# Fused attention, token-mixing MLP and residual on one core: order of the first loads, last transposes by halves, and a new table of dispatch tolerances

## The chip, the cores and the metric

The kernel runs on one core of a Trainium2 chip. The metric is the device time of one execution in microseconds (us). TensorE (PE in the profile) multiplies matrices, VectorE (DVE), ScalarE (ACT) and GpSimd (POOL) work elementwise, and SyncE (SP) issues most of the transfers; ScalarE issues a few. Each engine runs its own instructions in order and waits on semaphores for the others.

## The reference

```python
x = A_x                                  # 1 x 2048 x 512, bf16
xn = layernorm(x)
# A: attention, 32 heads of 16
q, k, v = split(xn @ wqkv)
p = softmax(q k^T / 4)
A = (p v) @ wo
# B: mixing along the 2048 tokens, F = 1376
h = layernorm(xn)
u = gelu(einsum("bsd,sf->bdf", h, w1) + b1)
B = transpose(einsum("bdf,fs->bds", u, w2) + b2)
out = x + A + B
```

## The kernel before

**Blocks and groups.** Attention is cut into 32 blocks: four blocks of 512 queries times eight sets of four heads. The four heads of a set share the 128 partitions, 32 rows each. A block runs over 16 key tiles of 128 keys, and one block with one key tile is a group, so there are 512 groups. For a group TensorE computes four score tiles, keys on the partitions and 512 queries along the free dimension, one PSUM bank per head (`score_mm`, L653).

**Two ways to the exponential.** ScalarE takes two heads at a time: one exponential of 128x1024 from two banks into a buffer `pT` (`exp_tile`, L661). VectorE has an approximation in integer arithmetic: four conversions of 128x512, one per head (`dve_first`, L708), then two "planes" of 128x2048, shifted copies of the first (`add_plane`, L713). The value products (`pv_mm`, L673) add a group into PSUM bank 6 as four matmuls for a group of ScalarE, twelve for a group of VectorE. The planes of VectorE's groups live in buffers that other work has left free: parts of `x_sb`, `xn_sb`, `xnT`, `wqkv_sb` and a buffer `plx`.

**Planning on the host.** The program is a list scheduler in Python. It keeps a model time for every engine and lets engines choose their next piece of work: `pe_step` for TensorE (scores for ScalarE if a pair of banks is nearly free, scores for VectorE, else `pe_fill`: value products "P", or pieces of projections and MLP "F"), `dve_step` for VectorE, `misc_step` for the others. Which engine takes a group comes out of this: `act_fetch` gives it to ScalarE, `d_fetch` to VectorE. The result is a fixed order for each engine, with semaphores where one depends on another. Twelve numbers steer the choices, for instance `TOL` (how much a filler on TensorE may overrun the time at which ScalarE's banks come free), `JOIN` and `DEFER` (whether VectorE's scores join ScalarE's, or TensorE waits for that), and `D_LAST` (until when VectorE may take groups of the last block). `POLICY` (L93) has 68 rows of them, one for each 10 us of model time.

**Head.** x is loaded in four single tiles of 128 rows (`NPRE`), in turn on the queues of SP and ScalarE, then in larger pieces on SP. `ld_w` (L478) loads weights: the first 128 columns of K (from SP), Q (from ScalarE) and V, later the rest. A small activation on ScalarE brings its table in. TensorE runs eleven products of zeros (`zeros`, L772) from the start. VectorE computes mean and variance of a tile (`ln_stats0` L525, `ln_aggr` L529), GpSimd the reciprocal root (`ln_stats2`: L541, then the power L543). Tile 0 is normalised by ScalarE (`ln_norm_act`, L547): GpSimd first computes its bias `r2` (L548), then ScalarE runs L550. Tiles 1 to 3 are normalised by VectorE (L559). TensorE transposes each tile (`transpose_mm`, L727), ScalarE or VectorE copies it to `xnT` (L588, L590), and K and Q of the four tiles are computed with 128-wide products (L594). ScalarE copies Q in four pieces (L614). After that the first scores and exponentials run, and the remaining twelve tiles follow in the gaps.

**Middle.** Projections, the first MLP product (L962), one GELU on ScalarE (L984), the second MLP product (L993) and the output projection (L1003) fill TensorE between scores and value products. At the end of a block VectorE copies the sums out (L1204), and their reciprocals go through DRAM back to all partitions.

**Tail.** The last block is finished on chip (`tail_epilogue`, L1848), in two halves of 256 columns, so that the output projection of a half can begin early. Each half has four VectorE steps: a transpose from bank 6 (L1862), a reciprocal (L1864), a product (L1866) and a transpose back (L1869). After a half, TensorE adds what that half opens to the last four output tiles (`op_half`, L1011); ScalarE or VectorE copies those out and they are stored. Products that do not depend on the last block wait in `tail["steps"]` and are put on TensorE where the model has room before the end of the half's last transpose.

Of the kernel before, what the change touches and what calls it, by code (L numbers as in the profile page):

```python
# [19 lines left out]
NT = S // 128  # L20
# [44 lines left out]
class Op:  # L65
# [25 lines left out]

SEG = 10000.0
POLICY = [  # L93
# [245 lines left out]
def bass_parallel_sum__softmax_full_mha__mixer_token_mlp__prompt_kernel(  # L339
# [11 lines left out]
    x = A_x  # L351
# [6 lines left out]
    with ExitStack() as es:  # L358
# [119 lines left out]
        def ld_w(j, T0_, T1_, lat, q="act"):  # L478
            c0, c1 = j * D + 128 * T0_, j * D + 128 * T1_
            dma(q, wqkv_sb[:, j, :, 128 * T0_:128 * T1_],  # L480
                A_wqkv[:, c0:c1].rearrange("(ct p) n -> p ct n", p=128),
                reads=[], writes=[("wqkv", j, T) for T in range(T0_, T1_)], name="ld_wqkv", lat=lat)

        for t in range(NPRE):
            dma(("sp", "act")[t % 2], x_sb[:, t, :], x2[128 * t:128 * t + 128, :], reads=[("ident",)] if t == 1 else [],
                writes=[("x", t)], name="ld_x", lat=2150 + 150 * t)
        ld_w(1, 0, 1, 3000, "sp")
        ld_w(0, 0, 1, 3100)
        sc.add("act", lambda e: e.activation(r2[:, 0:1], zw[:, 0:1], ACTF.Identity), reads=[("zw",)], writes=[("r2",)],
               occ=1500)  # L490
# [1483 lines left out]
```

## Time and profile before

| what | value |
|---|---|
| time, median of 3 runs | 691.82 us (690.92 to 692.32) |
| the profiled execution's own time | 693.56 us |
| its span in the profile | 691.5 us |
| busy: ScalarE / VectorE / TensorE / GpSimd | 675.3 / 661.2 / 652.0 / 68.6 us |
| exponentials on ScalarE (L661) | 720, 660.8 us busy |
| conversions on VectorE (L708), planes (L713) | 608, 304 |
| first exponential starts, last one ends | 14.25 us, 682.8 us |
| first transpose of the tail | 684.83 us |

Times are from the start of the span. An instruction's time in the profile can overlap the next one of the same engine, since the engines are pipelined. In a row of the timeline the first number is the start, the second the duration of the merged instructions, and the bracket at the end gives the engine's idle time before it and what released it. TensorE's granted clock reads 1.0 in all stages.

### The profile page before, as it was taken

Reading aid. Unit: us, or ns where it says so; the run is one execution under the profiler, and the core shown is the slowest. Engines: PE = TensorE matmul, PEld = TensorE weight load, DVE = VectorE, ACT = ScalarE, POOL = GpSimd, SP = SyncE. Lnnn points to the kernel's source line nnn. Section 1 sums busy time; section 2 is a strip of 40 time slices with the busy share of each in tenths; the row PEclk is TensorE's granted clock in tenths of the full one; section 3 lists DMA queues with packets and bytes.
Section 4 is the critical chain, followed back from the end, with each engine's and each line's share of the span. In section 5 each row is a group of like instructions: output and inputs, shape, how many; then the busy total and the mean of one; then the engine's idle time right before and its main releaser. Section 6 shows DMA issues by size and latency. Waiting matters only on the chain.

```text
span 691.5 us, 15523 instructions
## 1 busy us (share of the span) xinstructions
PE 652.0 (94%) x6197; PEld 201.6 (29%) x6285; DVE 661.2 (96%) x1159; ACT 675.3 (98%) x737; POOL 68.6 (10%) x100
## 2 busy tenths in 40 slices
PE   8999999999999999999999999999988999999987
PEld 4543333222222222222222222222222222222221
DVE  5988999999999999999999999999999999999997
ACT  4999999999999999999999999999999999999995
POOL 4620100000000000000000001000000000002010
PEclk9999999999999999999999999999999999999999
DMA  8024100122212211220022202211120122212001
GB/s 243 2 50 71 35 12 18 28 48 57 53 36 56 48 43 36 48 50 15 24 49 52 56 24 59 54 51 32 50 52 25 47 57 67 59 41 70 18 7 46
DMA packets 78367, 32.65 MB, mean 47 GB/s; under 512 B 63004, under 2 KB 74204, under 8 KB 78296
## 3 DMA queue, kind: packets, MB, share of 16 engines
q1 hardware_dynamic: 77336, 31.14, 18.7%
q8 instruction: 49, 0.80, 0.5%
q10 hardware_dynamic: 960, 0.52, 0.3%
q14 instruction: 22, 0.18, 0.1%
HBM read 26.08 MB, written 2.61 MB: 41 GB/s over the span
## 4 chain that ended last, share of the span: by engine, by line
ACT 86%; PE 9%; DVE 3%; DMA 1%; issue 1%; POOL 0%; POOLq 0%; DVEq 0%
ACT pT L661 84%; PE ps L673 3%; PE ps L653 3%; PE ps L962 1%; DVE plx L708 1%; ACT gT L984 1%; PE ps L993 1%; DVE x_sb L713 1%; DVE x_sb L708 1%; DMA x_sb<-in_A_x_dram 1%; PE ps L594 0%; PE ps L727 0%; DMA den_scr<-OT 0%; DMA den_s<-den_scr 0%; PE ps L1003 0%
## 5 line engine op out<-in xcount | busy, mean ns | idle before, releaser
L661 ACT ACTIVATE pT<-ps 128x1024 bf16<-128x1024 f32 x720 | 660.8, 1140 | 0.7 <-PE ps L653 0.6
L653 PE MATMUL ps<-QT,KT 32*128 32x512 bf16 x2048 | 288.3, 384 | 24.5 <-ACT pT L661 21.2
L708 DVE TENSOR_SCALAR plx<-ps 128x512 int16<-128x512 f32 x356 | 232.9, 679 | 5.5 <-PE ps L653 4.3
L708 DVE TENSOR_SCALAR x_sb<-ps 128x512 int16<-128x512 f32 x248 | 168.7, 683 | 7.0 <-PE ps L653 0.3
L653 PEld LDWEIGHTS ps<-QT,KT 32*128 32x128 bf16 x2048 | 73.1, 91 | 268.4 <-ACT pT L661 254.0
L673 PE MATMUL ps<-pT,V 128*32 128x512 bf16 x1440 | 142.5, 390 | 0.6 <-DVE V L590 0.3
L713 DVE TENSOR_SCALAR x_sb<-plx 128x2048 int16<-128x2048 int16 x143 | 96.2, 681 | 0.6 <-PE ps L673 0.2
L673 PE MATMUL ps<-plx,V 128*32 128x512 bf16 x624 | 60.4, 382 | 0.1
L673 PEld LDWEIGHTS ps<-pT,V 128*32 128x32 bf16 x1440 | 36.4, 93 | 80.3 <-issue 75.7
L673 PE MATMUL ps<-x_sb,V 128*32 128x512 bf16 x580 | 56.1, 382 | 0.4 <-DVE OT L1204 0.4
L1241 POOL TENSOR_TENSOR oT<-OT,denb 128x512 bf16<-128x512 f32 x16 | 20.3, 1271 | 335.4 <-DVE x_sb L713 188.7
L673 PE MATMUL ps<-x_sb,V17b 128*32 128x512 bf16 x532 | 52.2, 382 | 0.3 <-issue 0.3
L962 PE MATMUL ps<-h_sb,w1blk 128*128 128x512 bf16 (+1 forms) x152 | 49.8, 387 | 2.2 <-issue 2.2
L993 PE MATMUL ps<-gT,w2blk 128*128 128x512 bf16 (+1 forms) x151 | 49.0, 385 | 2.1 <-issue 1.9
L713 DVE TENSOR_SCALAR x_sb<-x_sb 128x2048 int16<-128x2048 int16 x72 | 49.4, 688 | 0.7 <-PE ps L673 0.7
L1241 POOL TENSOR_TENSOR otmp<-OT,denb 128x512 bf16<-128x512 f32 x15 | 19.1, 1273 | 247.4 <-DVE x_sb L713 128.2
L594 PE MATMUL ps<-xnT,wqkv_sb 128*128 128x512 bf16 (+1 forms) x169 | 37.9, 324 | 1.7 <-issue 1.4
L713 DVE TENSOR_SCALAR plx<-x_sb 128x2048 int16<-128x2048 int16 x51 | 34.7, 681 | 0.1
L713 DVE TENSOR_SCALAR plx<-plx 128x2048 int16<-128x2048 int16 x33 | 22.4, 680 | 0.1
L594 PE MATMUL ps<-wqkv_sb,xnT 128*128 128x128 bf16 x256 | 21.1, 220 | 0.0
L1204 DVE COPY OT<-ps 128x512 f32<-128x512 f32 x31 | 21.0, 677 | 0.0
L673 PEld LDWEIGHTS ps<-plx,V 128*32 128x32 bf16 x624 | 16.9, 96 | 12.9 <-issue 7.2
(96 smaller groups left out, 297.6 us busy)
## 6 DMA issues: line engine op xcount, KB each, us to landing
denb<-rec_scr SPq DMA_DIRECT2D x124, 64.0 KB, 2.1
w1blk<-in_B_w_dram SPq DMA_DIRECT2D x10, 512.0 KB, 4.2
w2blk<-in_B_w_dram SPq DMA_DIRECT2D x16, 320.0 KB, 3.7
xres<-in_A_x_dram SPq DMA_DIRECT2D x16, 128.0 KB, 2.3
QT<-qst SPq DMA_DIRECT2D x120, 16.0 KB, 1.8
out_dram<-osb SPq DMA_DIRECT2D x14, 128.0 KB, 1.7
wqkv_sb<-in_A_wqkv_dram SPq DMA_DIRECT2D x3, 384.0 KB, 7.8
x_sb<-in_A_x_dram SPq DMA_DIRECT2D x2, 512.0 KB
```

The costliest lines, as they stand in the source:

```text
L594: return sc.add("pe", lambda e: e.matmul(dst, lhsT=lhsT, rhs=rhs, start=(ct == 0), stop=(ct == NCT - 1)), reads=reads, writes=[("bank", bk ...
L653: return sc.add("pe", lambda e: e.matmul(bank(bk), lhsT=KT[32 * r:32 * r + 32, T, 128 * kt:128 * (kt + 1)], rhs=QT[32 * r:32 * r + 32, slo ...
L661: return sc.add("act", lambda e: e.activation(pT[:, buf, :], ps[:, slot * 1024:(slot + 1) * 1024], ACTF.Exp, scale=EXP_SCALE), reads=[("ba ...
L673: return sc.add("pe", lambda e: e.matmul(bank(PV_BANK)[32 * r:32 * r + 32, :], lhsT=vt_[:, off:off + 32], rhs=rhs, start=start, stop=stop, ...
L708: return sc.add("dve", lambda e: e.tensor_scalar(plane_i[pb][:, 512 * r:512 * (r + 1)], bank(bk), BIAS, 0.0, ALU.add, ALU.max), reads=[("b ...
L713: return sc.add("dve", lambda e: e.tensor_scalar(plane_i[pb], plane_i[pb0], float(SHIFT[j]), BITS_MAX, ALU.add, ALU.min), reads=[("pl", pb ...
L962: op = sc.add("pe", lambda e: e.matmul(bank(xb)[0:m, :], lhsT=w1blk[:, slot, st, 0:m], rhs=h_sb[:, st, :], start=(st == 0), stop=(st == NT ...
L984: op = sc.add("act", lambda e, m=m, f0=f0, f1=f1: e.activation(gT[0:m, f0:f1, :], gT[0:m, f0:f1, :], ACTF.Gelu_apprx_tanh), reads=[("gT", ...
L993: op = sc.add("pe", lambda e: e.matmul(bank(xb), lhsT=w2blk[0:m, slot, ft, :], rhs=gT[0:m, ft, :], start=first, stop=last), reads=([("w2bl ...
L1204: op = sc.add("dve", lambda e: e.tensor_copy(OT32[:, eb, :], bank(PV_BANK)), reads=[("bank", PV_BANK)], writes=[("OT32", eb)], **T_DVE(512))
L1241: op = sc.add("pool", lambda e: e.tensor_tensor(dst, OT32[:, eb, :], denb[:, :], ALU.mult), reads=[("OT32", eb)] + [("denb", r) for r in r ...
```

## The change

In the head, the first two tiles of x are loaded on SP's queue and the next two on ScalarE's. The first K weights follow on SP and wait there until tile 0 has arrived (a read of tile 0 is named as a dependency); the first Q weights come behind them on SP, no longer on ScalarE's queue. GpSimd's bias and ScalarE's norm of tile 0 are put ahead of the statistics of tile 1 in the engines' orders; the model's duration of that norm is 700 instead of 560 ns.

In the tail, the four VectorE steps run half by half in turn: both transposes, both reciprocals, both products, both transposes back. Buffers' keys are renamed accordingly.

In the planner, all rows of `POLICY` are replaced and get a thirteenth number, `SEED`; 38 of 68 rows have one that is not zero. A function `vary(j)` makes a fixed pseudo-random number between -1 and 1 from the seed, the count of exponentials so far and j. It shifts `TOL` by up to 50 ns, `JOIN` by up to 40 and `DEFER` by up to 100, and where `vary(3)` is over 0.6 (one time in five), a value product is ranked behind projection and MLP pieces in `pe_fill`. With seed 0 it gives 0.

```diff
 POLICY = [
-    (115.0, 80.0, 250.0, -1, 0, 1300.0, 0.0, 0.05, 2, 3, 2, 7500.0),
-    (90.0, 30.0, 150.0, -1, 0, 900.0, 0.0, 0.2, 2, 5, 0.9, 9500.0),
...
+    (115.0, 80.0, 250.0, -1, 0, 1300.0, 0.0, 0.05, 2, 3, 2, 7500.0, 0),
+    (95.0, 50.0, 250.0, -1, 0, 2000.0, 0.0, 0.0, 3, 3, 2, 10500.0, 63069),
...
-        def ld_w(j, T0_, T1_, lat, q="act"):
+        def ld_w(j, T0_, T1_, lat, q, after=()):
...
-                reads=[], writes=[("wqkv", j, T) for T in range(T0_, T1_)], name="ld_wqkv", lat=lat)
+                reads=list(after), writes=[("wqkv", j, T) for T in range(T0_, T1_)], name="ld_wqkv", lat=lat)
...
-            dma(("sp", "act")[t % 2], x_sb[:, t, :], x2[128 * t:128 * t + 128, :], reads=[("ident",)] if t == 1 else [],
-                writes=[("x", t)], name="ld_x", lat=2150 + 150 * t)
-        ld_w(1, 0, 1, 3000, "sp")
-        ld_w(0, 0, 1, 3100)
+            dma("sp" if t < 2 else "act", x_sb[:, t, :], x2[128 * t:128 * t + 128, :],
+                reads=[("ident",)] if t == 2 else [], writes=[("x", t)], name="ld_x", lat=2150 + 150 * t)
+
+        ld_w(1, 0, 1, 3000, "sp", [("x", 0)])
+        ld_w(0, 0, 1, 3100, "sp")
...
-                          reads=[("x", t), ("mvr", t), ("r2",)], writes=[("xn", t)], occ=560, lat=700)
+                          reads=[("x", t), ("mvr", t), ("r2",)], writes=[("xn", t)], occ=700, lat=810)
...
         zeros(11, 430)
         ln_stats(0)
+        ln_norm_act(0)
         ln_stats(1)
-        ln_norm_act(0)
         ln_stats(2)
...
+            f_first = vary(3) > 0.6
...
-                        order.append((0 if pv_press else 1, same, 0.0, c))
+                        order.append((0 if pv_press else 1, same, 99.0 if f_first else 0.0, c))
...
+        def vary(j):
+
+            if SEED == 0:
+                return 0.0
+            z = (SEED * 7919 + n_act_[0] * 104729 + j * 1299709 + 12345) & 0xffffffff
+            for _ in range(3):
+                z = ((z ^ (z >> 15)) * 0x2c1b3c6d) & 0xffffffff
+            return z / 2147483648.0 - 1.0
...
+                    join = max(0.0, JOIN + 40.0 * vary(1))
-                    if sw and t + 226.0 <= t_s + DEFER:
+                    if sw and t + 226.0 <= t_s + DEFER + 100.0 * vary(2):
...
-            lim = t_s + TOL if t_s is not None else 1e18
+            lim = t_s + TOL + 50.0 * vary(0) if t_s is not None else 1e18
...
+            for hf in range(2):
+                cols, blks, rc, dk, sk, wk = half(hf)
                 sc.add("dve", lambda e, cols=cols: e.transpose(denb[:, cols], bank(PV_BANK)[:, cols]),
...
+            for hf in range(2):
                 sc.add("dve", lambda e, rc=rc, blks=blks: e.reciprocal(rc, dn[:, blks, 16]), reads=[dk],
...
+            for hf in range(2):
                 sc.add("dve", lambda e, rc=rc, blks=blks: e.tensor_tensor(
...
+            for hf in range(2):
                 sc.add("dve", lambda e, cols=cols: e.transpose(otmp[:, po, cols], gT[:, 0, cols]), reads=[wk],
...
-                tr = sc.streams["dve"][-1].end
+            for hf in range(2):
+                tr = sc.streams["dve"][hf - 2].end
                 for z in list(tail["steps"]):
```

More of the change, by code (lines that the diff above doesn't have):

```diff
@@ L824, in bass_parallel_sum__softmax_full_mha__mixer_token_mlp__prompt_kernel @@
         pv_open = [True]
-        TOL, JOIN, DEFER, P1_PRI, D_PEND, FAR, D_HUNGRY, PACE, N_SAME, PRESS, PL_PRI, D_LAST = POLICY[0]
+        TOL, JOIN, DEFER, P1_PRI, D_PEND, FAR, D_HUNGRY, PACE, N_SAME, PRESS, PL_PRI, D_LAST, SEED = POLICY[0]
         kt_done = {0: 4}
@@ L1636, in pe_step @@
                     wait_d = False
-                    if sw and t + 226.0 <= t_s + DEFER:
+                    join = max(0.0, JOIN + 40.0 * vary(1))
+                    if sw and t + 226.0 <= t_s + DEFER + 100.0 * vary(2):
                         z = [sc.ready(writes=[("bank", k)]) if dbank[k] is None else (
                             max(sc.free["dve"], dbank[k][0]) + 740.0) for k in (4, 5, EX_BANK) if ex_active[k] is None]
-                        wait_d = bool(z) and min(z) > t + JOIN and min(z) <= t + 226.0 + JOIN and len(tp_done) == (NT - NPRE) // 2
+                        wait_d = bool(z) and min(z) > t + join and min(z) <= t + 226.0 + join and len(tp_done) == (NT - NPRE) // 2
                     if wait_d and pe_fill(t, t + 226.0, True):
@@ L1643, in pe_step @@
                     if t_s <= t + sw:
-                        frb = [k for k in d_room() if sc.ready(writes=[("bank", k)]) <= t + JOIN]
+                        frb = [k for k in d_room() if sc.ready(writes=[("bank", k)]) <= t + join]
                         act_fetch(len(frb))
@@ L1825, in bass_parallel_sum__softmax_full_mha__mixer_token_mlp__prompt_kernel @@
             while n_seg[0] * SEG <= t:
-                TOL, JOIN, DEFER, P1_PRI, D_PEND, FAR, D_HUNGRY, PACE, N_SAME, PRESS, PL_PRI, D_LAST = POLICY[min(n_seg[0], len(POLICY) - 1)]
+                TOL, JOIN, DEFER, P1_PRI, D_PEND, FAR, D_HUNGRY, PACE, N_SAME, PRESS, PL_PRI, D_LAST, SEED = POLICY[min(n_seg[0], len(POLICY) - 1)]
                 n_seg[0] += 1
@@ L1854, in tail_epilogue, with half @@
             wt = gT[:, 0, :].rearrange("p (c m) -> p c m", m=32)
+            def half(hf):
+                cols, blks = slice(256 * hf, 256 * hf + 256), slice(NB * hf, NB * hf + NB)
+                return (cols, blks, den_s[:, 0, blks], ("denT", hf), ("denS", hf), ("gTt", hf))
             for hf in range(2):
-                cols, blks = slice(256 * hf, 256 * hf + 256), slice(NB * hf, NB * hf + NB)
-                rc = den_s[:, 0, blks]
-                dk = ("denb", 0) if hf == 0 else ("denT", 1)
@@ L1860, in tail_epilogue @@
-                sk = ("den_s", 0) if hf == 0 else ("denS", 1)
-                wk = ("gT", 0) if hf == 0 else ("gTt", 1)
-                sc.add("dve", lambda e, cols=cols: e.transpose(denb[:, cols], bank(PV_BANK)[:, cols]),
-                       reads=[("bank", PV_BANK)], writes=[("denb", r) for r in range(4)] if hf == 0 else [dk], **T_DVE(256))
-                sc.add("dve", lambda e, rc=rc, blks=blks: e.reciprocal(rc, dn[:, blks, 16]), reads=[dk], writes=[sk],
-                       occ=180, lat=310)
+                cols, blks, rc, dk, sk, wk = half(hf)
@@ new lines, in tail_epilogue @@
+                sc.add("dve", lambda e, cols=cols: e.transpose(denb[:, cols], bank(PV_BANK)[:, cols]),
+                       reads=[("bank", PV_BANK)], writes=[dk] + ([("denb", r) for r in range(4)] if hf == 0 else []),
+                       **T_DVE(256))
+            for hf in range(2):
+                cols, blks, rc, dk, sk, wk = half(hf)
+                sc.add("dve", lambda e, rc=rc, blks=blks: e.reciprocal(rc, dn[:, blks, 16]), reads=[dk],
+                       writes=[sk] + ([("den_s", 0)] if hf == 0 else []), occ=100, lat=230)
@@ L1866, in tail_epilogue @@
+            for hf in range(2):
+                cols, blks, rc, dk, sk, wk = half(hf)
                 sc.add("dve", lambda e, rc=rc, blks=blks: e.tensor_tensor(
                     wt[:, blks, 0:16], dn[:, blks, 0:16], rc.rearrange("p (c o) -> p c o", o=1).broadcast_to([128, NB, 16]),
-                    ALU.mult), reads=[dk, sk], writes=[wk], **T_DVE(128))
+                    ALU.mult), reads=[dk, sk], writes=[wk] + ([("gT", 0)] if hf == 0 else []), **T_DVE(128))
+            for hf in range(2):
+                cols, blks, rc, dk, sk, wk = half(hf)
```

132 rows, old and new, of the table POLICY are left out of this document.

## The prediction

> **What bounds the kernel now.** I read first the page's busy shares and its chain of what ended last, to see which engine sets the time.
>
> ```profile
> PE 652.0 (94%) x6197; PEld 201.6 (29%) x6285; DVE 661.2 (96%) x1159; ACT 675.3 (98%) x737; POOL 68.6 (10%) x100
> ...
> ACT 86%; PE 9%; DVE 3%; DMA 1%; issue 1%; POOL 0%; POOLq 0%; DVEq 0%
> ...
> L661 ACT ACTIVATE pT<-ps 128x1024 bf16<-128x1024 f32 x720 | 660.8, 1140 | 0.7 <-PE ps L653 0.6
> ```
>
> ScalarE's 720 exponentials (two for each of 360 groups) are the time: 660.8 us with 0.7 us idle, 0.918 us each. So there are four things a change can move: when the first exponential starts, how many there are, how closely they follow each other, and what comes after the last. The busy share hides part of the third: an exponential is recorded as 1140 ns, overlapping the next, while their starts stand 0.904 us apart at the median. Over 720 that is 650.9 us, so some 10 us of short waits for scores are spread over the middle. VectorE has the other 152 groups (608 conversions at L708, 304 planes at L713).
>
> Then the start, in the timeline of the first 15 us, cut to the chain:
>
> ```profile
> 1.50 0.91 ACTq L431 DMA_DIRECT2D x_sb<-in_A_x_dram  x2
> 2.88 0.69 DVE L525 BATCH_NORM_STATS2 stats<-x_sb 128x6 f32<-128x512 bf16 x1 [1.65 <-DMA x_sb<-in_A_x_dram]
> 5.01 0.69 DVE L525 BATCH_NORM_STATS2 stats<-x_sb 128x6 f32<-128x512 bf16 x1 [1.23 <-DMA x_sb<-in_A_x_dram]
> 6.32 0.57 POOL L543 TENSOR_TENSOR mv<-mv,mhalf 128x1 f32<-128x1 f32 x1
> 6.99 0.27 POOL L548 TENSOR_SCALAR r<-mv 128x1 f32<-128x1 f32 x1
> 7.29 0.81 ACT L550 ACTIVATE xn_sb<-x_sb,r,mv 128x512 bf16<-128x512 bf16 x1 [2.86 <-POOL r L548]
> 8.16 0.61 PE L727 MATMUL ps<-ident,xn_sb 128*128 128x128 bf16 x4 [2.02 <-ACT xn_sb L550]
> 10.70 3.19 PE L594 MATMUL ps<-xnT,wqkv_sb 128*128 128x128 bf16 x28
> 12.22 1.57 ACT L614 ACTIVATE QT<-ps,qmask 128x384 bf16<-128x384 f32 x4 [1.43 <-PE ps L594]
> 14.14 0.62 PE L594 MATMUL ps<-wqkv_sb,xnT 128*128 128x128 bf16 x8
> 14.25 8.36 ACT L661 ACTIVATE pT<-ps 128x1024 bf16<-128x1024 f32 x9 [0.46 <-PE ps L653]
> ```
>
> Tile 0 of x is in by 2.88, yet its norm on ScalarE starts at 7.29: its bias r, at 6.99, is queued on GpSimd behind tile 1's power (6.32), and tile 1, first on ScalarE's queue, lands only at 5.0. From 8.16 TensorE is the chain. Last, the end of the same view:
>
> ```profile
> 684.83 0.45 DVE L1862 STREAM_TRANSPOSE denb<-ps 128x256 f32<-128x256 f32 x1 [0.83 <-PE ps L673]
> 685.32 0.20 DVE L1864 RECIPROCAL den_s<-denb 128x8 f32<-128x8 f32 x1
> 685.55 0.29 DVE L1866 TENSOR_TENSOR gT<-denb,den_s 128x128 bf16<-128x128 f32 x1
> 685.88 0.45 DVE L1869 STREAM_TRANSPOSE otmp<-gT 128x256 bf16<-128x256 bf16 x1
> 686.25 0.41 DVE L1862 STREAM_TRANSPOSE denb<-ps 128x256 f32<-128x256 f32 x1
> 687.25 0.45 DVE L1869 STREAM_TRANSPOSE otmp<-gT 128x256 bf16<-128x256 bf16 x1
> 687.76 0.61 PE L1011 MATMUL ps<-wo_pad,otmp 128*128 128x512 bf16 x2
> ```
>
> After the last group's value product, two halves of four VectorE steps run one after the other.
>
> **Head: loads.** Tile 1 takes the second place on SP's queue, where tile 2 was: issue 1.19, landing 2.5 later (SP's two single tiles have a median of 2.3 to landing and the shortest 2.1), so 3.7 instead of 5.0. Tiles 2 and 3 take ScalarE's queue at 1.50 and 1.96; at today's 3.5 there they would be in at 5.0 and 5.5, needed at 4.5 and 5.3. But half of that 3.5 was shared with weights that now wait for tile 0, and GpSimd (below) is later still, so I cost this at nothing; bound 0 to 0.3. The new wait stands on SP: the first K weights go at 2.9 instead of 1.65, and behind them queue Q's weights (3.4, on ScalarE's queue at 2.44 before), x tiles 4 to 15, V's and the other weights, each 1.75 later. With today's 4.1 to 4.8 to landing, K's are in at 7.0 to 7.7 and Q's at 7.5 to 8.2, and wanted at 8.0 and 8.8 (below); tiles 4 and 5 with today's 4.6 at 8.5, wanted at 9.3. All covered, by 0.3 us at the least; a transfer that is later than that delays the first exponential one for one. ScalarE's own first instructions come 0.46 earlier, covered.
>
> **Head: the norm at once.** The bias of tile 0 no longer follows tile 1: the first power ends at 4.76, r runs 4.86 to 5.13, ScalarE's norm 5.16 to 5.98, 2.1 earlier. But TensorE's eleven warming products hold its queue until 5.93, so transposes of tile 0 start at 6.03, just behind. VectorE's statistics of tiles 1 to 3 go from 3.70 at the recorded 0.81 a tile, 1.3 earlier. GpSimd then has tile 1's power at 5.5, tile 2's at 6.45, tile 3's until 7.57 (8.72 now); VectorE's norms end at 6.7, 7.5 and 8.0 (9.18 now).
>
> **Head: TensorE.** At the recorded 107 ns per 128-wide product: tile 0 6.03, zero 6.46, tile 1 6.89, tile 2 (its norm) 7.53, K 7.96, tile 3 8.39, then Q and K, 28 x 0.107 from 8.82. ScalarE's four copies of Q began 0.35 after the twelfth of these and take 1.57: 10.35 to 11.92; scores to exponential 0.43: first exponential at 12.4, a gain of 1.9. The rows show another speed too: 28 products took 3.19 us until 13.9, eight took 0.62 from 14.14, 56 ns apart. TensorE had then worked without a break for 5.6 us; the 4.9 us from 1.26 had not been enough, and 2 us of rest followed. The new order leaves almost no rest after 1.26, so 5.6 us are over at 6.9. With 56 ns from there the norms bound it: tile 3's transposes 8.06, Q's copies from about 9.0, first exponential near 10.7, a gain of 3.5. The Trainium skill ("TensorE: Matmul & The Clock Gate", Part 1) says the array starts at half rate and is released after one busy window of about 3.4 us, free-running, so its phase differs from run to run; by that the sum would use 3.5, while a lucky phase today would already be fast. No run here shows the phase.
>
> The middle follows the head: the ninth exponential needs K of tiles 4 and 5, whose copy ends at 20.45, 0.4 before its scores start at 20.9; that chain starts at tile 4's statistics and K's copy, which move by the same 2 to 3.5.
>
> **The planner's numbers.** All 68 rows of POLICY are new, 38 with a seed that shifts tolerances by at most 40, 50 or 100 ns, and in those one choice in five prefers a filler over a value product. No instruction is added; order, and possibly the split of groups, changes. A group moved to VectorE saves two exponentials, 1.835 us, and costs it 4 + 2 slots of 0.6 = 3.6 us; VectorE's idle time between 24 and 685 us is about 20 us, 7.5 of it before 100, so there is room for one or two at most, and nothing forces any. The short waits of 10 us may become 8.5 or 11.5. I take zero for both, bounds -3.7 and +3.7.
>
> **Tail.** The second half's steps run in the first's shadow: starts at 684.83, 685.20, 685.55, 685.70, then the products, then transposes at 686.2 and 686.56, done 687.0 instead of 687.7; the first half is done at 686.65 instead of 686.33. TensorE has three products between the halves' pairs; if they all stay between, 686.70 + 5 x 0.215 = 687.78 and nothing is won; with one moved ahead 0.2, with all three 0.6. I take 0.2.
>
> **Sum.** The profiled execution took 693.56 (span 691.5 and 2.06 around it), 1.74 over the median of 691.82. Head 1.9 to 3.5, tail 0.2: 689.9 to 691.5 against the profiled one. Its slow head may be part of the 1.74 (the timed runs show no head), and then they have less to gain from the faster clock; against the median I take 2.4 for the head: 691.82 - 2.4 - 0.2 = 689.2, own range 688.1 to 690.4.
>
> **Rivals.** (1) The fast clock at full worth in every run: 691.82 - 3.7 = 688.1, down to 687.5 with the tail; for it the unbroken 5.6 us, against it the 4.9 us that did not suffice. (2) More groups go to VectorE: 687.4 with one, 685.5 with two; for it 7.5 us idle before 100, against it 98% busy later. (3) The head's gain is handed back: one group more on ScalarE, or 1.8 us more of waits: 691.0, at most 692; a measurement cannot tell less than 0.2%, 1.4 us, from no change. (4) Slower: VectorE loses groups in the middle, because the jittered tolerances let it run dry and ScalarE takes them. Each costs 1.835; the head's 2.6 pays for one, with two it is 692.9, from three on 694.7 and plainly slower. For it only that VectorE today waits just 4.3 us on scores in all, so it has much to lose. (5) The loads change nothing, because tile 1 lands at 5 on SP too: then the bias alone gains nothing either, since tiles 2 and 3 still bind, 691.5; tile 2's landing from that place speaks against it.
>
> **Numbers.** Forecast 0.45, (1) 0.13, (2) 0.14, (3) and (5) 0.16, (4) 0.12, counted as three groups or as much in waits. Faster holds the forecast but for 0.02 of it, (1) and (2): 0.70; same 0.18; slower 0.12. The range reaches from one to two groups more (686.0) to (3) and a little of (4), 692.4.
>
> **What would show it.** Tile 1's statistics at 3.7, r at 4.9, norms done by 8.0, first exponential between 10.6 and 12.4; 720 exponentials at 0.918; the last transpose 2.2 after the first. Wrong if the count at L661 is not 720, if exponentials are further than 0.92 apart on average, or if TensorE waits for weights before 9 us.

## The result, and the profile after

The changed kernel takes 689.57 us (median of 11 runs, 689.12 to 690.82) against 691.82 us (11 runs, 690.85 to 693.85): a ratio of 0.9973 with the interval [0.9962, 0.9984]. The forecast was 689.2. Its profiled execution took 689.35 us with a span of 687.1, against 693.56 and 691.5.

The page after, in the order of the first fence of the prediction: busy shares, the chain by engine, and the group of exponentials (count | busy, mean ns of one | idle before).

```profile
PE 649.8 (95%) x6200; PEld 197.5 (29%) x6287; DVE 660.6 (96%) x1159; ACT 675.5 (98%) x737; POOL 68.3 (10%) x100
...
ACT 84%; PE 11%; DVE 3%; issue 1%; DMA 0%; POOL 0%; DVEq 0%
...
L663 ACT ACTIVATE pT<-ps 128x1024 bf16<-128x1024 f32 x720 | 661.0, 1128 | 0.7 <-PE ps L655 0.5
```

ScalarE still sets the time, with the same 720 exponentials and the same 661 us. (Up to the tail, line numbers are one or two higher than before.) The split of groups did not move. What moved lies at both ends. The timeline of the head after:

```profile
1.50 0.86 ACTq L432 DMA_DIRECT2D x_sb<-in_A_x_dram  x2
2.89 0.94 SPq L432 DMA_DIRECT2D wqkv_sb<-in_A_wqkv_dram  x2
2.90 0.69 DVE L527 BATCH_NORM_STATS2 stats<-x_sb 128x6 f32<-128x512 bf16 x1 [1.67 <-DMA x_sb<-in_A_x_dram]
3.73 0.66 DVE L527 BATCH_NORM_STATS2 stats<-x_sb 128x6 f32<-128x512 bf16 x1
4.88 0.27 POOL L550 TENSOR_SCALAR r<-mv 128x1 f32<-128x1 f32 x1
5.18 0.81 ACT L552 ACTIVATE xn_sb<-x_sb,r,mv 128x512 bf16<-128x512 bf16 x1 [1.29 <-POOL r L550]
6.05 0.45 PE L729 MATMUL ps<-ident,xn_sb 128*128 128x128 bf16 x4
8.21 1.75 PE L596 MATMUL ps<-xnT,wqkv_sb 128*128 128x128 bf16 x28
9.08 1.57 ACT L616 ACTIVATE QT<-ps,qmask 128x384 bf16<-128x384 f32 x4 [0.68 <-PE ps L596]
9.97 0.39 PE L655 MATMUL ps<-QT,KT 32*128 32x512 bf16 x2
10.52 11.21 ACT L663 ACTIVATE pT<-ps 128x1024 bf16<-128x1024 f32 x12
```

The second tile's statistics start at 3.73 instead of 5.01, r at 4.88 instead of 6.99, the norm at 5.18 instead of 7.29, and tile 0's transposes at 6.05 without a wait of TensorE before them. The 28 products of K and Q take 1.75 us instead of 3.19, and the first exponential starts at 10.52 instead of 14.25. The tail after, from VectorE's last plane on:

```profile
678.36 0.69 DVE L715 TENSOR_SCALAR x_sb<-plx 128x2048 int16<-128x2048 int16 x1
678.65 1.14 ACT L663 ACTIVATE pT<-ps 128x1024 bf16<-128x1024 f32 x1
679.77 0.47 PE L675 MATMUL ps<-pT,V 128*32 128x512 bf16 x4
680.28 0.78 DVE L1875 STREAM_TRANSPOSE denb<-ps 128x256 f32<-128x256 f32 x2 [1.23 <-PE ps L675]
681.59 0.76 DVE L1889 STREAM_TRANSPOSE otmp<-gT 128x256 bf16<-128x256 bf16 x2
682.08 0.60 PE L1013 MATMUL ps<-wo_pad,otmp 128*128 128x512 bf16 x2
682.52 0.38 PE L1005 MATMUL ps<-wo_c,oT 128*128 128x512 bf16 x1
682.74 0.59 PE L1043 MATMUL ps<-gT,ident 128*128 128x512 bf16 x2
683.17 0.38 PE L1013 MATMUL ps<-wo_pad,oT 128*128 128x512 bf16 x1
683.39 0.59 PE L1013 MATMUL ps<-wo_pad,otmp 128*128 128x512 bf16 x2
684.02 0.60 ACT L590 ACTIVATE xres<-ps 128x512 bf16<-128x512 f32 x1 [0.42 <-PE ps L1013]
```

Between the two pairs of `otmp` products stand four others, at 682.52 to 683.17. Before, ScalarE's last exponentials and VectorE's last plane were these:

```profile
675.15 7.65 ACT L661 ACTIVATE pT<-ps 128x1024 bf16<-128x1024 f32 x8
...
683.31 0.69 DVE L713 TENSOR_SCALAR x_sb<-plx 128x2048 int16<-128x2048 int16 x1
```

Put together, the two spans differ by four terms:

| stage | before | after | difference |
|---|---|---|---|
| start to first exponential | 14.25 | 10.52 | -3.73 |
| first exponential's start to last one's end | 668.55 | 669.27 | +0.72 |
| that end to the tail's first transpose | 2.03 | 0.49 | -1.54 |
| first transpose to the end of the span | 6.64 | 6.82 | +0.18 |
| span | 691.47 | 687.10 | -4.37 |

The median moved by only 2.25 us. The runs below show that the same kernel before can begin its exponentials 3 us earlier than in this profile.

### The profile page after: what moved, and what is told of

Same layout as the page of the kernel before. It is cut to its first block, busy times and chain, and to the rows that moved or that the text cites. A ratio compares the mean times of both kernels' runs of the same rounds, so it can differ in the third digit from the quotient of the medians.

```text
span 687.1 us, 15560 instructions
## 1 busy us (share of the span) xinstructions
PE 649.8 (95%) x6200; PEld 197.5 (29%) x6287; DVE 660.6 (96%) x1159; ACT 675.5 (98%) x737; POOL 68.3 (10%) x100
## 4 chain that ended last, share of the span: by engine, by line
ACT 84%; PE 11%; DVE 3%; issue 1%; DMA 0%; POOL 0%; DVEq 0%
ACT pT L663 84%; PE ps L655 4%; PE ps L675 4%; PE ps L995 1%; DVE x_sb L710 1%; DVE plx L710 1%; PE ps L964 1%; DVE x_sb L715 1%; DVE plx L715 1%; PE ps L1712 0%; DMA x_sb<-in_A_x_dram 0%; PE ps L1005 0%; PE ps L1013 0%; DVE stats L527 0%; PE ps L596 0%
## 5 line engine op out<-in xcount | busy, mean ns | idle before, releaser
L710 DVE TENSOR_SCALAR plx<-ps 128x512 int16<-128x512 f32 x344 | 225.0, 678 | 2.6 <-PE ps L655 1.6
L710 DVE TENSOR_SCALAR x_sb<-ps 128x512 int16<-128x512 f32 x244 | 166.1, 683 | 7.0 <-PE ps L655 0.8
L715 DVE TENSOR_SCALAR x_sb<-plx 128x2048 int16<-128x2048 int16 x135 | 91.3, 683 | 0.3
L675 PE MATMUL ps<-plx,V 128*32 128x512 bf16 x592 | 56.9, 382 | 0.5 <-issue 0.5
L675 PE MATMUL ps<-x_sb,V17b 128*32 128x512 bf16 x484 | 47.5, 383 | 0.8 <-issue 0.3
L715 DVE TENSOR_SCALAR x_sb<-x_sb 128x2048 int16<-128x2048 int16 x65 | 44.1, 682 | 0.4 <-PE ps L675 0.4
L715 DVE TENSOR_SCALAR plx<-x_sb 128x2048 int16<-128x2048 int16 x54 | 37.6, 696 | 0.3 <-PE ps L675 0.3
L596 PE MATMUL ps<-xnT,wqkv_sb 128*128 128x512 bf16 (+1 forms) x166 | 34.5, 305 | 2.1 <-issue 1.6
L995 PEld LDWEIGHTS ps<-gT,w2blk 128*128 128x128 bf16 (+1 forms) x176 | 12.4, 97 | 25.5 <-issue 22.1
L964 PEld LDWEIGHTS ps<-h_sb,w1blk 128*128 128x128 bf16 (+1 forms) x176 | 12.4, 99 | 25.3 <-issue 22.6
```

The source lines that it names most:

```text
L596: return sc.add("pe", lambda e: e.matmul(dst, lhsT=lhsT, rhs=rhs, start=(ct == 0), stop=(ct == NCT - 1)), reads=reads, writes=[("bank", bk ...
L675: return sc.add("pe", lambda e: e.matmul(bank(PV_BANK)[32 * r:32 * r + 32, :], lhsT=vt_[:, off:off + 32], rhs=rhs, start=start, stop=stop, ...
L710: return sc.add("dve", lambda e: e.tensor_scalar(plane_i[pb][:, 512 * r:512 * (r + 1)], bank(bk), BIAS, 0.0, ALU.add, ALU.max), reads=[("b ...
L715: return sc.add("dve", lambda e: e.tensor_scalar(plane_i[pb], plane_i[pb0], float(SHIFT[j]), BITS_MAX, ALU.add, ALU.min), reads=[("pl", pb ...
L964: op = sc.add("pe", lambda e: e.matmul(bank(xb)[0:m, :], lhsT=w1blk[:, slot, st, 0:m], rhs=h_sb[:, st, :], start=(st == 0), stop=(st == NT ...
L995: op = sc.add("pe", lambda e: e.matmul(bank(xb), lhsT=w2blk[0:m, slot, ft, :], rhs=gT[0:m, ft, :], start=first, stop=last), reads=([("w2bl ...
```

## The experiments

Each kernel has 12 timed runs (p1 and p3 six), interleaved with 29 to 35 runs of before on the same chip. "Full clock" is the median span of those executions whose mean granted clock read 0.9985 or more, with their number; it is given because executions of one kernel differ in that (last part of this section). The four runs from h1 to h4 shared one chip, t1 to p1 another, k1 to p3 a third.

| run | median us (range) | ratio to before, interval | full clock | first exponential |
|---|---|---|---|---|
| h1 | 691.74 (690.51 to 693.31) | 0.9999 [0.9988, 1.001] | 689.45 (10) | 12.44 |
| h2 | 690.94 (689.83 to 692.12) | 0.9984 [0.9973, 0.9995] | 688.9 (11) | 12.38 |
| h3 | 689.74 (689.16 to 691.15) | 0.9972 [0.9961, 0.9982] | 687.55 (10) | 12.22 |
| h4 | 690.65 (689.35 to 692.59) | 0.9982 [0.997, 0.9994] | 687.9 (7) | 11.50 |
| t1 | 689.37 (688.77 to 690.29) | 0.9968 [0.9952, 0.9983] | 687.1 (8) | 10.71 |
| t2 | 689.40 (689.07 to 691.09) | 0.9967 [0.995, 0.9983] | 687.2 (12) | 10.47 |
| t6 | 689.06 (688.82 to 690.89) | 0.9969 [0.9953, 0.9986] | 687.0 (12) | 10.71 |
| p1 | 701.20 (700.27 to 703.15) | 1.0135 [1.0108, 1.0162] | 698.5 (3) | 10.57 |
| k1 | 690.17 (689.51 to 690.82) | 0.9967 [0.9951, 0.9982] | 688.2 (12) | 10.72 |
| a1 | 689.69 (689.08 to 691.06) | 0.9965 [0.9948, 0.9981] | 687.1 (8) | 10.51 |
| r1 | 690.64 (690.18 to 693.17) | 0.9983 [0.9967, 0.9999] | 688.6 (11) | 11.25 |
| p3 | 700.47 (699.47 to 702.02) | 1.0116 [1.009, 1.0141] | none | 13.80 |

Before itself, on the three chips: 692.17, 691.29 and 692.23 us; at full clock 689.2 (19 of 35), 688.1 (17 of 29) and 688.7 (13 of 29).

**Head, TensorE's speed: h1 and h2.** The question was how much of the 3.73 us is TensorE's faster products rather than the earlier norm. h1 is before with five more products of zeros, meant to keep TensorE busy through its rest; h2 is the changed kernel with a rest put in.

```diff
# h1, in before
-        zeros(11, 430)
+        zeros(16, 430.0 * 11 / 16)
# h2, in the changed kernel
-        zeros(11, 430)
+        zeros(4, 430.0 * 11 / 4)
```

> The kernel before, with 16 instead of 11 products of zeros at the start (they end at about 8.1 us, where tile 0's transposes begin); the order and the model times are otherwise the same. Theory A (half of the head's gain is TensorE's speed, which needs an unbroken start): TensorE is at 56 ns per 128-wide product from 8.2 us, the norms of tiles 2 and 3 (8.7 and 9.2) then bind, first exponential at about 11.9 instead of 14.25, time 2.0 to 2.4 us below the profiled kernel before. Rival B (the gain is the loads and the norm alone): first exponential stays at 14.2, time unchanged within 0.3 us. Either way 720 exponentials.

> The changed kernel with 4 instead of 11 products of zeros, model times the same, so TensorE rests from about 3.0 to 6.05 us. Theory A: 107 ns per 128-wide product through the head, first exponential at 12.4 (the sum of the prediction at the slow speed) instead of 10.52, the profiled time 1.9 us more. Rival B: the speed comes by itself by 6.2 us, first exponential at 10.5, no change.

The timeline of h1, tile 0's transposes, the products of K and Q and the first exponentials:

```profile
8.58 0.40 PE L727 MATMUL ps<-ident,xn_sb 128*128 128x128 bf16 x4 [2.38 <-ACT xn_sb L550]
...
10.13 1.75 PE L594 MATMUL ps<-xnT,wqkv_sb 128*128 128x128 bf16 x28
...
12.44 2.87 ACT L661 ACTIVATE pT<-ps 128x1024 bf16<-128x1024 f32 x3
```

The same stretch of h2:

```profile
6.12 0.61 PE L729 MATMUL ps<-ident,xn_sb 128*128 128x128 bf16 x4 [2.97 <-ACT xn_sb L552]
8.95 3.06 PE L596 MATMUL ps<-xnT,wqkv_sb 128*128 128x128 bf16 x28
12.38 2.85 ACT L663 ACTIVATE pT<-ps 128x1024 bf16<-128x1024 f32 x3 [0.33 <-PE ps L655]
```

h1 did not do what it was meant to: its products of zeros turned fast at 3.96 us, while the seventh was running (before has eleven of the same), so the sixteen ended at 6.20 and TensorE rested 2.38 us all the same. It stayed fast through that rest. h1 is therefore no test of the rest, but it shows before's loads and norm with the fast speed: the 28 products take 1.75 us, and the first exponential starts 1.8 earlier than in the profile of before, although the second tile landed at 5.44, against 5.0 in that profile. In h2, with early loads and norm but 2.97 us of rest, the 28 products take 3.06 us and the first exponential starts at 12.38: the 12.4 that the prediction worked out for the slow speed. So 1.9 us of the 3.73 is the loads and the norm, and 1.9 is the speed. Yet h1's time is that of before, although its profile's head is 1.8 shorter. Its profiled span of 689.55 is typical of its executions at full clock (689.45), and before's at full clock have 689.2, against 691.5 in the profile: most of these cannot have had the profiled one's head.

**Head, its two parts: h3 and h4.** h3 keeps the changed kernel's whole order, but puts tile 0's bias and norm back behind tile 1's power; h4 keeps it, but puts the loads back on their former queues and without the wait for tile 0.

```diff
# h3
-        ln_norm_act(0)
-        ln_stats(1)
+        norm0, bias0 = ln_norm_act(0), sc.streams["pool"][-1]
+        pow1 = ln_stats(1) or sc.streams["pool"][-1]
...
+        behind(bias0, pow1)      # moved after planning
+        behind(norm0, bias0)
# h4, after planning
+        x0, x1, x2_, x3, wk, wq = sc.dma_ops[:6]
...
+        wk.deps = [d for d in wk.deps if d is not x0]
+        for op, q in ((x1, "act"), (x2_, "sp"), (wq, "act")):
...
```

> The changed kernel, only GpSimd's bias of tile 0 (and ScalarE's norm) again behind tile 1's power; all other orders as they are. Theory A: bias at about 5.9 instead of 4.9, norm of tile 0 ends at 7.0 instead of 6.0; TensorE rests 1 us; with the fast speed from then on the first exponential is 0.4 to 0.6 later (11.0), with the slow speed 2.4 later (12.9). Rival C (the norm's place is worth its whole 2.1 us, since tile 0 heads the chain): first exponential 2.1 later at the fast speed. Rival D (nothing, tiles 2 and 3 bind): 10.5.

> The changed kernel with the loads of before (tiles 0 and 2 on SP, 1 and 3 on ScalarE's queue, K's weights not waiting, Q's on ScalarE's queue); all other orders as they are, the norm of tile 0 still ahead. Theory A: tile 1's statistics at 5.0 instead of 3.7, the norms of tiles 1 to 3 about 0.8 later, a rest of TensorE of about 1.5 us at 6.5; first exponential at 11.3 at the fast speed, 13.5 at the slow one, as the rest leaves it. Rival D (the loads are worth nothing): 10.5.

The timeline of h3, from r to the first exponentials:

```profile
5.67 0.27 POOL L550 TENSOR_SCALAR r<-mv 128x1 f32<-128x1 f32 x1
...
6.84 0.61 PE L729 MATMUL ps<-ident,xn_sb 128*128 128x128 bf16 x4 [0.70 <-ACT xn_sb L552]
...
9.38 2.25 PE L596 MATMUL ps<-xnT,wqkv_sb 128*128 128x128 bf16 x28
...
12.22 2.87 ACT L663 ACTIVATE pT<-ps 128x1024 bf16<-128x1024 f32 x3
```

The same of h4:

```profile
5.03 0.69 DVE L527 BATCH_NORM_STATS2 stats<-x_sb 128x6 f32<-128x512 bf16 x1 [1.26 <-DMA x_sb<-in_A_x_dram]
...
8.10 0.72 PE L729 MATMUL ps<-ident,xn_sb 128*128 128x128 bf16 x8 [1.18 <-DVE xn_sb L561]
...
11.50 3.79 ACT L663 ACTIVATE pT<-ps 128x1024 bf16<-128x1024 f32 x4
```

Without the norm's new place r comes 0.8 later, TensorE rests 0.70, and in the profiled execution its products turned fast only at 10.5: the first exponential is 1.7 later. This execution (span 688.9) is one of the two slowest of h3's ten at full clock (median 687.55), so no profile shows what the norm's place costs at the fast speed. Without the new loads the second tile's statistics wait until 5.03, and TensorE waits 1.18 for its norm; products were fast, and the first exponential is 1.0 later. The loads are thus worth about 1 us of head against this landing, and the norm's place more than that only where the speed comes late. At full clock h4 is slower than a1 by 0.8 and h3 by 0.45, on different chips.

**Tail: t1, t2, t6.** t1 is the changed kernel with the former order of the halves. t2 lets every independent product go ahead of the first half's pair. t6 is t2 with two tiles' last identity products left to VectorE's addition.

```diff
# t2
-                    while z and (z[0][0] in TBANK[2 * hf:2 * hf + 2] or sc.free["pe"] + 226.0 <= tr):
+                    while z:
# t6, besides
-                if c in HL:
+                if c == 3:
...
+        gone = [o for o in sc.streams["pe"] if o.name in ("part0", "part1")]
```

> The changed kernel with the tail's four VectorE steps again one half after the other; everything ahead of the tail is the same. Theory A (TensorE's queue sets the tail's end: between the first half's pair and the second half's stand four products of 0.215): the first pair 0.3 earlier, the second half's last transpose ends 0.8 later (T0 + 2.9), the last pair within 0.2 of T0 + 3.1, time within 0.3 us of the changed kernel. Rival E (the order of the halves is worth the 0.7 us that VectorE saves): 0.6 to 0.7 us slower.

> The changed kernel with the four products that do not depend on the last block put ahead of the first half's pair. Theory A (the tail is TensorE's sixteen products of 0.215 after the last value product, with 0.2 us of idle time among them): the pairs stand together, the last output copy ends 0.1 to 0.2 earlier, time the same. Rival E (VectorE's last transpose sets the end): 0.6 earlier.

> As t2, and the partial sums of the first two of the four last output tiles are added by VectorE as it copies them out, where the changed kernel adds them by two identity products each and ScalarE copies: four products less in all, two of them after the last value product. Theory A: the last pair 0.6 us earlier than in the changed kernel, last copy ends 0.6 earlier. Against it: VectorE now copies three of four tiles, 0.6 each, which could take the lead: then 0.3 or nothing.

The timeline of t1, the second half's last transpose and its products:

```profile
682.97 0.45 DVE L1882 STREAM_TRANSPOSE otmp<-gT 128x256 bf16<-128x256 bf16 x1
...
683.62 0.59 PE L1013 MATMUL ps<-wo_pad,otmp 128*128 128x512 bf16 x2
```

The end of the timeline of t6:

```profile
682.14 1.03 PE L1013 MATMUL ps<-wo_pad,otmp 128*128 128x512 bf16 x4
...
683.21 0.60 ACT L590 ACTIVATE xres<-ps 128x512 bf16<-128x512 f32 x1 [3.61 <-PE ps L1013]
683.76 0.68 DVE L1905 TENSOR_TENSOR xres<-ps,h_sb 128x512 bf16<-128x512 f32 x1
```

Counted from the first transpose, the second half's last transpose ends after 2.87 us in t1 and after 2.07 in the changed kernel, 0.8 earlier; the last pair of products begins after 3.07 and 3.11, and ScalarE's last copy ends after 4.30 and 4.34. The 0.8 us are real and buy nothing: TensorE still has its queue of some sixteen products, 0.215 us each, behind the last value product. With all of them ahead (t2, last copy after 4.48) the pairs merely wait for the queue; with two tiles' products removed (t6) the pairs begin 2.06 instead of 2.49 after the first transpose, but VectorE, which now copies three tiles, ends after 4.36. TensorE, VectorE and ScalarE share this end to within 0.2 us. t6 has the lowest median, but its interval overlaps those of t1, t2 and a1.

**The table: p1, p3, k1.** p1 is the changed kernel with before's 68 rows and no seeds, planned anew. p3 is its opposite: the new rows with before's loads and order of the norm. k1 is before's planned order to the last instruction, with only the new loads and the place of the norm put in after planning.

```diff
# p1
-    (95.0, 50.0, 250.0, -1, 0, 2000.0, 0.0, 0.0, 3, 3, 2, 10500.0, 63069),
+    (90.0, 30.0, 150.0, -1, 0, 900.0, 0.0, 0.2, 2, 5, 0.9, 9500.0, 0),
...
# p3
-        ld_w(1, 0, 1, 3000, "sp", [("x", 0)])
+        ld_w(1, 0, 1, 3000, "sp")
...
# k1, in before, after planning
+        behind(bias0, pow0)
+        behind(norm0, bias0)
+        wk.deps = wk.deps + [x0]
+        for op, q in ((x1, "sp"), (x2_, "act"), (wq, "sp")):
...
```

> The changed kernel with the 68 rows of before and no seeds; head and tail as changed. Theory A (the head is its own gain and the table is worth little): first exponential at 10.5, 720 exponentials, the stretch from first to last within 1 us of 669.3, and after it 0.5 to 2 us more until the first transpose of the tail: 0 to 2 us slower than the changed kernel. Rival F (the new table is what brings the gain): 722 to 726 exponentials or a stretch 2 us or more longer, no faster than before. Rival G (the table is a loss that the head hides): 1 us or more faster than the changed kernel.

> The changed kernel with the head of before in the program (loads, order of the norm, the model's duration of it), planned anew with the new table and the new tail. Theory A (a table fits only the course of events it was made for; the one before cost 11.6 us on the new head): more than 720 exponentials or a longer end, 2 to 12 us slower than before. Rival J (the new table is better by itself): 0.5 to 1 us faster than before.

> The kernel before with its whole planned order kept, and only the head moved after planning as in the change: tiles 0 and 1 on SP, 2 and 3 on ScalarE's queue, K's first weights waiting for tile 0, Q's on SP, bias and norm of tile 0 ahead of tile 1's statistics. Theory A (the head's gain goes to the end one for one, and the new table with the tail is worth little on top): first exponential at 10.5 to 10.7, stretch of the exponentials 668.5, 2.0 us from the last of them to the tail's first transpose, span 687.8; time 2.0 to 2.6 us below before, within 0.8 us of the changed kernel. Rival H (the table carries most of the gain): under 1 us below before.

The group of exponentials of p1:

```profile
L663 ACT ACTIVATE pT<-ps 128x1024 bf16<-128x1024 f32 x726 | 666.7, 1135 | 2.3 <-PE ps L655 2.2
```

The same of p3:

```profile
L663 ACT ACTIVATE pT<-ps 128x1024 bf16<-128x1024 f32 x728 | 669.4, 1120 | 1.6 <-PE ps L655 1.6
```

The same of k1:

```profile
L661 ACT ACTIVATE pT<-ps 128x1024 bf16<-128x1024 f32 x720 | 660.8, 1140 | 0.1
```

A table fits only the head that it stands with. With the wrong rows ScalarE has three or four groups more (726 and 728 exponentials): their stretch is 676.5 us in p1 and 678.4 in p3. In p1 the tail's first transpose comes another 6.4 us after the last exponential, since VectorE is still at work on its groups. p1, expected to cost 0 to 2 us, is 11.8 slower than t1 and 9.9 slower than before on its chip; p3 is 8.2 slower than the interleaved runs of before and 9.8 slower than r1. The new rows are thus no improvement that would work alone; mostly they restore what planning anew on the new head would have upset. k1 avoids that by keeping the plan. Three lines of its timeline, the last exponentials, the last plane and the tail's first transpose:

```profile
677.11 2.10 ACT L661 ACTIVATE pT<-ps 128x1024 bf16<-128x1024 f32 x2
...
679.73 0.69 DVE L713 TENSOR_SCALAR x_sb<-plx 128x2048 int16<-128x2048 int16 x1
...
681.25 0.45 DVE L1862 STREAM_TRANSPOSE denb<-ps 128x256 f32<-128x256 f32 x1 [0.83 <-PE ps L673]
```

The last exponential ends at 679.21 and the first transpose follows 2.03 later, as in before: VectorE converts for its last group until 679.1 and ends that group's second plane at 680.42, 1.2 behind ScalarE. In the changed kernel it ends its last plane at 679.05, 0.7 ahead of ScalarE, and only the last exponential's own value products stand between (0.49). t1, with the former order of the halves, has 0.49 too, so this is the table's doing and not the tail's. Between the profiles of k1 and a1, spans 687.9 and 686.9, the new table and tail give 1.54 at this place, lose 0.55 in the stretch of exponentials (668.49 to 669.04) and 0.20 in the tail, and the head differs by 0.22. At full clock the executions say the same: 688.2 for k1, 687.1 for a1. Of the seeds alone nothing was tried.

**How much the head is worth: a1 and r1.** Both kernels unchanged, in the batch of k1, with the runs of before interleaved.

> The changed kernel once more, beside the others on the same chip: 689.2 to 690.0, first exponential at 10.5 to 10.7.

> The kernel before once more, for where TensorE's speed changes. Theory A (the start of the fast speed wanders from run to run, since it came 2.7 to 5.8 us after the start of unbroken work in the kernels so far): first exponential either near 12 or at 13.5 to 14.3, with the rest the same as in the first profile. Rival I (it is fixed): 14.2 again.

Three lines of the timeline of r1, tile 1's statistics, the products of K and Q and the first exponentials:

```profile
4.25 0.69 DVE L525 BATCH_NORM_STATS2 stats<-x_sb 128x6 f32<-128x512 bf16 x1 [0.37 <-DMA x_sb<-in_A_x_dram]
...
8.94 1.75 PE L594 MATMUL ps<-xnT,wqkv_sb 128*128 128x128 bf16 x28
...
11.25 5.61 ACT L661 ACTIVATE pT<-ps 128x1024 bf16<-128x1024 f32 x6
```

The same kernel that began its exponentials at 14.25 begins them here at 11.25: its second tile landed at 4.25 and its products were fast by 6.8. In all seven profiles with the new head and all eleven products of zeros (the changed kernel, a1, t1, t2, t6, p1, k1) they begin between 10.47 and 10.72. The new head gains 0.5 to 0.8 us against this good execution of before and 3.5 to 3.8 against the bad one.

How often each occurs, the times tell in part. At full clock k1 gains 0.4 to 0.5 on before (688.6 in r1, 688.7 interleaved), and the changed kernel 1.5 to 1.6. The rest of the difference of the medians comes from executions of before whose mean clock is lower: 44 of the 93 interleaved ones, with spans some 1.5 to 2.2 us longer on each chip, against 7 of 23 of the changed kernel and none of k1's 12. But r1, the very same program as before, has one of 12, and its median is 1.6 us under the interleaved runs in the same batch: a ratio of 0.9983 whose interval leaves out 1 arises here without any change. By r1 the change gains 0.95 us, by the interleaved runs 2.54. Which of before's executions fall into that half, and whether the head has a part in it, stays open. p3's profile shows one way in which it could: with before's loads and norm its TensorE was fast from 6.2, rested 2.4 us and then ran at half the clock from 9.6 to 13.0, so that its exponentials began at 13.80. One such stretch of 3.4 us takes 0.0025 off the mean clock of a whole execution, and 35 of the 44 low ones read 0.997 or 0.998; that their stretch lies in the head is not shown.

## Why the prediction was right or wrong

**The loads: right.** Tile 1's statistics at 3.73 (3.7 forecast). The tile itself was in at 3.37, earlier than the sum had it; VectorE's work on tile 0 set the start. The covers held with room to spare: the first Q weights landed at 6.72 (7.5 to 8.2 forecast), x tiles 4 and 5 at 7.40 (8.5), and nothing on TensorE waited for weights before 9 us. Tiles 8 to 15 landed 2.1 later than before (12.15 and 13.69) without being felt.

**The norm: right to 0.02 us.** r at 4.88 (4.86), norm at 5.18 (5.16), transposes at 6.05 (6.03).

**TensorE: both ends right, and the choice between them hedged.** At the slow speed 12.4 was forecast and h2 gives 12.38; at the fast one 10.7, and 10.52 came. The way from "about 9.0" to 10.7 is not written out: with the slow sum's own steps, 1.57 for the four copies of Q and 0.43 for the scores, it would have been 11.0. The scores did not wait for all four copies, which ran from 9.08 to 10.65; they began at 9.97. The argument from 5.6 us of unbroken work put the switch at 6.9; it came at 6.2 here and between 4.7 and 7.3 in the others, and within that span it does not matter, since the norms bind. The Trainium skill ("TensorE: Matmul & The Clock Gate", Part 1) says that the rate is released after one busy window of about 3.4 us that runs freely, so that its phase differs from run to run. The runs agree in kind: 2.7 us (h1) to 6.0 us (a1) after the start of unbroken work, for the same products; h1's 2.7 is less than the 3.4 of that rule, and the measurement decides. The prediction named as the other side of this rule that a lucky phase would make before fast already; r1's 11.25 is that case, with a landing 0.76 earlier besides, and h1 is another.

**The head's 2.4 on the median: the doubt was right, the size is not settled.** That the profiled execution's slow head was part of its excess over the median was forecast, and r1 and h1 bear it out. The head alone (k1) measured 2.06 under the interleaved runs of before, and 0.47 under r1. At full clock, where only the head differs, it is 0.4 to 0.5: there the 2.4 is five times too large, and it hits the median only with the help of before's low-clock executions, of which the sum knew nothing. That 689.2 came within 0.4 us of 689.57 is therefore in part luck: at full clock the whole change is worth 1.5 to 1.6 us, and the larger part of that (1.1, from k1 to a1) comes with the new table from the end of the last block, which the forecast did not price.

**The planner's numbers: the bounds held, the zero did not quite.** "Nothing forces any" group was right, 720 stayed. But the sum looked only at how closely exponentials follow each other, and not at what VectorE still has to do after the last one: that was -1.54, against +0.72 in the middle. The 2.03 us stood in the profile of before, as 682.8 and 684.83, with the first transpose's bracket naming the value products.

**The tail's 0.2: wrong, it is nothing.** The second half's last transpose ended 2.07 after the first began (2.2 forecast), but that was not what the end waited for. The step says what is needed for it, "with one moved ahead 0.2"; none was, and there were four between the pairs, not three. The lower bound, "nothing is won", was the answer, and t1 shows it.

**The rivals.** (1) The fast clock at full worth happened in the profile (-3.73) and not on the median. (Its lower value counts the tail's 0.2 twice: 691.82 - 3.5 - 0.6 is 687.7, not 687.5.) (2) and (4), groups moving either way, did not happen; p1 shows that (4)'s three groups are what a table does that does not fit its head, at 11.8 us rather than 5.5, because the end goes out of balance too. (3): some was handed back, 0.72 in the middle, not all. (5) is refuted by 3.73.

## What to carry to other kernels

In a plan where one engine is 98% busy, read the end as closely as the start: which engine finishes its last piece last, and by how much. When a profile's head or tail looks slow, look at a second execution before pricing it, since the gain against the one that was profiled can be several times the gain against a typical one. And a table of planned choices belongs to the times that it was made for: measure an edit of the head with the old plan kept, as in k1, or the plan's own change of 10 us hides it.

## What the runs showed of the hardware that was not expected

TensorE's clock can be halved again, not only start low. Two windows of p3 (columns: busy PE, PEld, DVE, ACT, POOL with counts, granted clock, DMA share, GB/s):

```profile
6.20:9.60 3.40, 1.02 (x13) 0.77 (x13) 2.96 (x9) 1.41 (x3) 2.36 (x6) 1.00 1.10 327
9.60:13.00 3.40, 3.37 (x33) 3.34 (x33) 1.63 (x4) 1.76 (x7) 1.50 (x4) 0.50 1.10 334
```

After 3.4 us with only 1.02 busy, the next 3.4 ran at half the clock. The same happened in r1 in the middle of the kernel, while ScalarE was in its GELU (331.2 to 336.2):

```profile
334.50:344.70 10.20, 10.20 (x35) 1.93 (x34) 7.41 (x12) 8.02 (x8) 0.00 (x0) 0.50 0.09 24
```

That execution's stretch of exponentials is 671.29 us, against 668.55 in the profile of before, so 10.2 us at half the clock cost 2.7. It was the same program, and the profile of before stays at full clock in that place. TensorE's work is thin there (11 products in the 3.4 us ahead, 31 in the 3.4 before those); that this set off the half clock, in one execution and not in the other, is an inference. Within the span, the half-clock stretches of r1, p1 and p3 last 3.41 us or three times that, but for those that begin in the last microsecond. A rest of the same length did not always cost the speed: p3's 2.4 us fell into one such stretch (1.02 us busy, above); h1's 2.38 us, counted in steps of 3.41 from the start of its record, fell into two, 3.96 to 7.38 and 7.38 to 10.79, with 2.25 and 2.18 us busy. That this is why h1 stayed fast is a reading of two executions, not a test. The column of the granted clock is no guide in the head of before: it reads 1.00 there while 28 products take 3.19 us, where fast ones take 1.75. The trace's own record of the clock begins only with the first full-speed stretch, at 13.79 us in before, 11.74 in h2, 10.46 in h3, 6.83 in r1, 6.20 in the changed kernel and 3.96 in h1. Ahead of that the speed has to be read from durations, and the two agree.

The landing of tile 1 moved from 4.25 to 5.44 us between five executions with before's loads (r1 and h1 at the ends; 5.01, 5.03 and 5.43 in before, h4 and p3), which is more than the new head gains on a good execution of before.
